# Sums by TensorE in 32-column strips, weight splitting on VectorE, and a new order, in a fused attention and gated MLP kernel

## The chip, the cores and the metric

The kernel runs on one core of a Trainium2 chip. The core has five engines that run side by side, each through its own instructions in order: TensorE (PE, matrix products), VectorE (DVE), ScalarE (ACT), GpSimd (POOL), and SyncE (SP), which here issues the transfers (DMAs). They wait for each other by semaphores. SBUF is the on-chip memory with 128 partitions; PSUM holds what TensorE produces. The metric is the time of one execution on the device in microseconds, the median of several runs. "Busy" times and instruction times come from one execution taken with the hardware profiler.

## The reference

Batch 8, 12 heads, 448 positions, head size 64; model width 768, inner width 1024, all in fp32.

```python
scores = cap * np.tanh(scale * (q @ k.T) / cap)
scores = scores - np.max(scores, axis=-1, keepdims=True)
attn = np.exp(scores)
attn = attn / (np.sum(attn, axis=-1, keepdims=True) + 1e-09)
x = attn @ v                                # heads side by side: (8, 448, 768)
h = np.maximum(x @ w_in, 0.0)               # 768 -> 1024
u, v = h[..., :512], h[..., 512:]
v_n = (v - mean(v)) / np.sqrt(var(v) + 1e-06)          # over the 512
v_s = np.einsum('ts,bsd->btd', w_spatial, v_n) + b_spatial[None, :, None]
out = (u * v_s) @ w_out                     # 512 -> 768
```

The weights w_in and w_out come as float64; cap is a scalar that is known only at run time.

## The kernel before, in words

**Two bodies.** `either` loads cap and the first q, k tiles (`raws`, L902 to L904), keeps TensorE busy with `WARM` = 14 matmuls on zeros (L909), and branches on cap (L920). For a cap up to a bound the body with `bounded=True` runs, the one measured here: the scores are bounded, so exp is taken without subtracting the maximum first, and the maximum only serves the small term 1e-09 in the denominator.

**Attention by quads** (`quad_bnd`). Four heads are one quad; a batch has three, the kernel 24 (`turn` 0 to 23). A q, k tile `raw` holds two heads, 448 columns of q and 448 of k in each partition. For each of the 7 blocks of 64 keys, four 64x64 matmuls (L594), one for each quarter of TensorE's array, make the scores of four heads with the keys on the partitions; ScalarE takes tanh of the block (L598) and exp of two blocks at a time in place (L605) in one of six `tp` buffers; four quadrant matmuls a block (L615) sum the product with v in PSUM (`ps_x`), and ScalarE copies it out (L621).

**Maxima and sums.** For all quads DVE folds the exps of the 7 blocks elementwise (L633), transposes in 32x32 blocks (L641) and reduces (L643), once for the maximum and once for the sum. For the first `PE_SUMS` = 3 quads the sum is made by TensorE instead: quadrant matmuls with a 64x64 tile of ones (L662), accumulated into two PSUM tiles, two ScalarE copies (L671), and four small transfers into `dt` (L674), where the denominators are made (L683, L685). They are written to memory (L686) and read back broadcast (L689), and DVE multiplies (L698). `halves` splits each product into a high part (ACT, L355) and a low part (DVE, L351), both in the reduced format fp32r.

**The MoE part** (`moe`, once a batch) multiplies such split operands in three matmuls per product: with w_in (L754 to L756, L776 to L781), with w_spatial (L845 to L850), with w_out (L870 to L872), on the full 128x128 array. It needs all three quads of its batch and the weights split. For the first of them `FILL` = 8 filler matmuls (L753) come ahead.

**The weights** are loaded as pairs of 32-bit words and turned from float64 into fp32 by `split_f64`: a scaling of the upper word (on GpSimd, L420), three integer steps on DVE (L424, L425, L427), the high part (ACT) and the low part (DVE). `E_W = "PAV"` names the engines of the scaling, the high and the low part. w_in comes in 12 pieces of 512 columns, w_out in 12 of 256; w_spatial, already fp32, in four, with the low parts on GpSimd (L383).

**The order.** Each piece of work is a task with engine, estimated duration, dependences, the buffers it takes and a key. `Plan.order` plays the tasks through once as the program is built: an engine that is free takes, of the tasks that are ready and have buffers, the one with the lowest key; on TensorE a task of the other kind ("R": quadrants, "N": full array) has `STICK` added to its key, and a change costs `TURN`. The order found is fixed in each engine's instruction stream. The keys come from `BND_KEY`, `BND_ADJ` (one for each quad or batch and kind) and `BND_W_KEYS` (the weights).

Of the kernel before, what the change touches and what calls it, by code (L numbers as in the profile page):

```python
# [18 lines left out]
FH = DF // 2  # L19
# [8 lines left out]
def f(ap):  # L28
    return ap.bitcast(F32)
# [13 lines left out]
class Plan:  # L43
# [8 lines left out]
    TURN, STICK = 180.0, 5.6142  # L52
# [131 lines left out]
HW, HH, XL = 400, 620, 50  # L184
# [19 lines left out]
def dve(n):  # L204
    return 1.06 * n + 70
# [40 lines left out]
BND_KEY = dict(ld=20.2062, vld=16.3748, sc=-4.4101, th=2.6266, ex=-12.5751, pv=3.8334, sm=4.9568, mx=1.2536,  # L246
               dn=-1.9573, ev=0.5509, x=0.5743, moe=3.5126, span=11.5964, step=-1.1271, mv=-7.699, vld_=0.5863, sc_=0.1716,
               th_=0.234, ex_=3.1048, pv_=-0.3915, sm_=-0.1418, mx_=1.5249)
BND_ADJ = dict(sc0=-1.9208, sc1=-0.6751, sc2=-0.5665, sc3=0.6591, sc4=1.0022, sc5=0.9243, sc6=0.5641, sc7=3.5286,
               sc8=4.1291, sc9=2.1364, sc10=0.4432, sc11=-0.3562, sc21=1.0782, sc22=-2.0787, sc23=-1.8651, mx0=7.5468, mx1=4.1712,  # L250
               mx2=0.2306, mx3=-3.4986, mx4=-4.2501, mx5=-7.8699, mx6=-6.59, mx7=-4.2274, mx8=-1.6152, mx9=-1.0965, mx10=-2.503,
               mx11=2.4712, mx21=3.6487, mx22=7.5152, mx23=10.1101, sm0=-23.9232, sm1=-5.9121, sm2=-19.3382, sm3=-4.1068,
               sm4=-7.6692, sm5=-6.9113, sm6=-7.6076, sm7=-2.9296, sm8=-4.8786, sm9=-2.9017, sm10=0.1476, sm11=-1.028,
               sm21=7.8004, sm22=5.003, sm23=9.0892, dn0=-13.9326, dn1=2.5665, dn2=1.5054, dn3=3.678, dn4=5.4586, dn5=2.0101,
               dn6=-0.9345, dn7=1.341, dn8=5.2032, dn9=5.9753, dn10=6.5428, dn11=-0.3824, dn21=0.2627, dn22=-7.9155, dn23=32.9005,
               x0=-1.8155, x1=-12.9607, x2=-3.0392, x3=-3.3476, x4=1.7459, x5=0.4945, x6=3.9029, x7=6.1809, x8=0.3782, x9=6.0115,
               x10=5.0057, x11=0.7894, x21=7.5672, x22=-1.7504, x23=1.6104, moe0=-2.1731, moe1=4.7513, moe2=2.8101, moe3=2.4916,
               moe7=9.0071, span0=-2.667, span1=-3.3859, span2=-2.449, span3=-5.6885, span7=28.8127, mv0=4.9503, mv1=-2.4788,
               mv2=2.6326, mv3=3.2084, mv7=-12.8989, wi0=-3.2806, wi1=-21.6066, wi2=-37.6263, wi3=14.5167, wi4=16.5614,
               wi5=1.1376, wi6=13.0344, wi7=2.468, wi8=-18.9783, wi9=3.3202, wi10=-13.2504, wi11=-12.154, ws0=-12.654,  # L260
               ws1=-7.9959, ws2=-33.2129, ws3=-10.2049, wo0=-6.4452, wo1=-0.8201, wo2=2.6051, wo3=8.6589)
BND_V_FIRST = 1
WARM, WARM_N, FILL = 14, 512, 8
BND_W_KEYS = -14.6272, 0.1578, -3.1507, 14.803, -4.1788, 0.5729, 0.2535
SPARE = ()
PE_SUMS = 3
E_W = "PAV"
# [6 lines left out]
def attn_moe(ctx, tc, bounded, shared, qk, v, qk2, v2, cap, w_in, w_sp, w_out, out):  # L274
# [33 lines left out]
    ic, ca, nca, half, raws = shared  # L308
    own = {"raw": list(raws)}
# [63 lines left out]
    def split_f32(key, c):  # L373
# [9 lines left out]
        l = [add("P", gp(S), key, lambda: sub("P", lo[:n], t.t[:n, :S], f(hi[:n])), [b], [t])]  # L383
# [17 lines left out]
    def split_f64(key, src, hi, lo, n, late=False):  # L401


        if late:
            w = y = Buf("xg")
        else:
            w, y = Buf("w64"), Buf("wy")
        y0 = 2 * n if late else 0
# [4 lines left out]
        t = add("S", HW, key, lambda: nc.sync.dma_start(out=w.t.bitcast(U32)[:, :2 * n], in_=src), allocs=[w], lat=dm(128, 8 * n))  # L413
# [18 lines left out]
        for i, (e, d, fn) in enumerate(ops):  # L432
            t = add(e, d, key, fn, [t], [w, y] if i < 4 else [y], [y] if i == 0 and not late else [], name="w64")
# [8 lines left out]
    for j in range(2):  # L442
        for c in range(NP):
            wi_t.append(split_cols((W_KEYS[0] + c * W_KEYS[1], W_KEYS[5] + c * W_KEYS[6])[j] + adj("wi", j * NP + c), j * FH, (j + 1) * FH, lambda key, i, n, c=c, j=j: split_f64(
                key, wi32[c * 128:(c + 1) * 128, 2 * i:2 * n], (wi1_h, wi2_h)[j][:, c, i - j * FH:n - j * FH], (wi1_l, wi2_l)[j][:, c, i - j * FH:n - j * FH], n - i)))
# [119 lines left out]
    def quad_bnd(b, n):  # L565
# [55 lines left out]
        z = add("A", act(PW, 1), kk("ev"), lambda: nc.scalar.copy(out=two(xf.t), in_=x.t[:, :, :S]), [prev], [x, xf], [xf], name="xev")  # L621
# [273 lines left out]
def either(ctx: ExitStack, tc: tile.TileContext, *args):  # L895
# [7 lines left out]
    for i, r in enumerate(raws):  # L903
        nc.sync.dma_start(out=r, in_=args[2][0, i])  # L904
# [14 lines left out]
    shared = ic, ca, nca, half, raws  # L919
# [35 lines left out]
```

## Time and profile before

| | |
|---|---|
| median of 3 runs | 728.85 us (728.6 to 729.24) |
| profiled execution: span, first to last instruction | 726.5 us |
| PE busy | 713.2 us (98%), 4910 matmuls |
| DVE busy | 600.4 us (83%) |
| ACT busy | 479.9 us (66%) |
| POOL busy | 78.4 us (11%) |
| mean granted clock of TensorE | 0.997 |

The profiled execution's own time is its span and what lies around it; the median of the timed runs is 2.35 us longer than the span. Matmuls are pipelined: each is shown with its whole passage through the array, so that PE counts as busy where it could take more, and the spacing of starts says more than the duration of one. An fp32 matmul appears as two matmul records, one in fp32r as one.

### The profile page before, as it was taken

The numbers are of one execution on the slowest core, as the hardware profiler recorded it, in microseconds if no ns is written. First come the engines' busy times: TensorE is split into PE (matmuls) and PEld (weight loads), VectorE is DVE, ScalarE is ACT, GpSimd is POOL, SyncE is SP. The second block draws the span as 40 slices with busy tenths as digits, with TensorE's granted clock in tenths as the row PEclk, the third lists the DMA queues.
The fourth block names the chain that finished last, engine by engine and source line by source line (L and its number), as shares of the span: only waits on it lengthen the run. The fifth ranks groups of instructions, "written<-read, shape, count | busy, mean of one in ns | idle before, by whom it ended". The sixth has DMA issues, their size and how long they took to land.

```text
span 726.5 us, 12274 instructions
## 1 busy us (share of the span) xinstructions
PE 713.2 (98%) x4910; PEld 487.7 (67%) x4910; DVE 600.4 (83%) x849; ACT 479.9 (66%) x648; POOL 78.4 (11%) x71
## 2 busy tenths in 40 slices
PE   8998999999999999999999999999999999999997
PEld 3333576575668657785568688568566865699896
DVE  4899999999999989948999996299799778983520
ACT  6999757849883894649875833786876678424321
POOL 1234310600110001000120001000021000200100
PEclk9999999999999999999999999999999999999999
DMA  8564314524221431033321430124321131202002
GB/s 279 165 204 148 129 38 134 168 80 142 85 78 30 149 129 49 28 91 114 102 76 28 153 103 27 49 66 141 102 77 41 47 131 39 53 2 101 1 1 80
DMA packets 34263, 66.50 MB, mean 92 GB/s; under 512 B 6034, under 2 KB 21908, under 8 KB 34196
## 3 DMA queue, kind: packets, MB, share of 16 engines
q1 hardware_dynamic: 34196, 65.62, 28.3%
q8 instruction: 40, 0.66, 0.4%
q14 instruction: 27, 0.22, 0.1%
HBM read 54.40 MB, written 11.18 MB: 90 GB/s over the span
## 4 chain that ended last, share of the span: by engine, by line
PE 79%; DVE 12%; issue 4%; ACT 2%; DMA 1%; SPq 1%; POOL 0%; DVEq 0%; ACTq 0%; POOLq 0%
PE ps_s L594 13%; PE ps_x L615 13%; PE ps_acc L870 5%; PE ps_acc L871 5%; PE ps_acc L872 5%; PE ps_acc L754 4%; PE ps_acc L756 4%; PE ps_acc L755 4%; DVE red L633 4%; PE ps_acc L779 4%; PE ps_acc L780 3%; PE ps_acc L781 3%; PE ps_acc L848 2%; PE ps_acc L850 2%; PE ps_acc L849 2%
## 5 line engine op out<-in xcount | busy, mean ns | idle before, releaser
L598 ACT ACTIVATE tp<-ps_s,capt 128x896 f32<-128x896 f32 x168 | 162.2, 1003 | 28.6 <-PE ps_s L594 18.1
L633 DVE TENSOR_TENSOR red<-red,tp 128x1792 f32<-128x1792 f32 x90 | 140.9, 1566 | 22.5 <-ACT tp L605 20.8
L605 ACT ACTIVATE tp<-tp,capt 128x1792 f32<-128x1792 f32 (+1 forms) x96 | 154.0, 1606 | 1.5
L594 PE MATMUL ps_s<-raw 64*64 64x448 f32 x1344 | 147.1, 545 | 3.6 <-ACT tp L598 3.5
L615 PE MATMUL ps_x<-tp,v 64*64 64x448 f32 x1344 | 140.0, 536 | 0.5 <-ACT tp L605 0.4
L633 DVE TENSOR_TENSOR red<-tp 128x1792 f32<-128x1792 f32 x45 | 91.2, 2027 | 13.9 <-ACT tp L605 13.0
L615 PEld LDWEIGHTS ps_x<-tp,v 64*64 64x64 f32 x1344 | 51.3, 133 | 75.7 <-issue 68.2
L594 PEld LDWEIGHTS ps_s<-raw 64*64 64x64 f32 x1344 | 47.1, 132 | 80.1 <-issue 46.5
L803 POOL TENSOR_TENSOR lst<-lst,capt 128x1 f32<-128x1 f32 x32 | 34.9, 1091 | 526.7 <-DVE lst L801 482.9
L754 PE MATMUL ps_acc<-xg,wi_h 128*128 128x448 f32 x180 | 66.2, 368 | 0.5 <-ACT xg L355 0.5
L755 PE MATMUL ps_acc<-xg,wi_h 128*128 128x448 f32 x180 | 65.3, 363 | 0.7 <-DVE xg L351 0.6
L756 PE MATMUL ps_acc<-xg,wi_l 128*128 128x448 f32 x180 | 65.2, 362 | 0.0
L870 PE MATMUL ps_acc<-xg,wo_h 128*128 128x448 f32 x176 | 64.5, 367 | 0.0
L871 PE MATMUL ps_acc<-xg,wo_h 128*128 128x448 f32 x176 | 63.7, 362 | 0.6 <-DVE xg L351 0.6
L872 PE MATMUL ps_acc<-xg,wo_l 128*128 128x448 f32 x176 | 63.8, 362 | 0.0
L355 ACT CAST xg<-o 128x448 fp32r<-128x448 f32 x32 | 18.1, 566 | 55.0 <-DVE o L855 49.5
L641 DVE STREAM_TRANSPOSE red<-red 128x896 f32<-128x896 f32 x45 | 49.6, 1102 | 0.7
L779 PE MATMUL ps_acc<-wi_h,xg 128*128 128x512 f32 x126 | 50.1, 398 | 0.0
L643 DVE TENSOR_REDUCE st<-red 128x28 f32<-128x896 f32 x45 | 48.6, 1079 | 0.7
L780 PE MATMUL ps_acc<-wi_l,xg 128*128 128x512 f32 x126 | 49.1, 390 | 0.0
L781 PE MATMUL ps_acc<-wi_h,xg 128*128 128x512 f32 x126 | 49.1, 390 | 0.0
L633 DVE TENSOR_TENSOR red<-red 128x896 f32<-128x896 f32 x45 | 48.6, 1079 | 0.6
(146 smaller groups left out, 1110.1 us busy)
## 6 DMA issues: line engine op xcount, KB each, us to landing
raw<-in_qk SPq DMA_DIRECT2D x48, 448.0 KB
rr<-rd SPq DMA_DIRECT2D x48, 224.0 KB
out<-o SPq DMA_DIRECT2D x48, 224.0 KB
w<-in_w_in SPq DMA_DIRECT2D x12, 512.0 KB
v<-in_v SPq DMA_DIRECT2D x24, 256.0 KB
v<-in_v SPq DMA_DIRECT2D x24, 192.0 KB
xg<-in_w_out SPq DMA_DIRECT2D x12, 256.0 KB
rd<-dt SPq DMA_DIRECT2D x48, 3.5 KB
```

The costliest lines, as they stand in the source:

```text
L594: nc.tensor.matmul(ps.t[c * D:(c + 1) * D, e, :S], lhsT=f(raw[c].t)[r, k:k + D], rhs=f(raw[c].t)[r, :S], start=True, stop=True)
L598: th = add("A", act(PW, 1), kk("th", i), lambda ps=ps, tp=tp, o=o: nc.scalar.activation(out=tp.t[:, o:o + PW].rearrange("p (e q) -> p e q" ...
L605: ex = add("A", act_s(w, 1), kk("ex", i), lambda tp=tp, w=w: nc.scalar.activation(out=tp.t[:, :w], in_=tp.t[:, :w], func=AF.Exp, scale=ca) ...
L615: nc.tensor.matmul(x.t[e * D:(e + 1) * D, c, :S], lhsT=vts[g // 2].t[c * D:(c + 1) * D, (4 * (g % 2) + 2 * j + e) * D:(4 * (g % 2) + 2 * j ...
L633: nc.vector.tensor_tensor(o_(), i0(), i1(), op=op)
L754: nc.tensor.matmul(ps, lhsT=wi1_h[:, c, fs], rhs=x[:, XH:], start=(c == 0), stop=False)
L755: nc.tensor.matmul(ps, lhsT=wi1_h[:, c, fs], rhs=x[:, :S], start=False, stop=False)
L756: nc.tensor.matmul(ps, lhsT=wi1_l[:, c, fs], rhs=x[:, XH:], start=False, stop=(c == NP - 1))
L779: nc.tensor.matmul(ps, lhsT=x[:, XH:][:, ts], rhs=wi2_h[:, c], start=(c == 0), stop=False)
L870: nc.tensor.matmul(ps, lhsT=wo_h[:, c, ns], rhs=g[:, XH:], start=(c == 0), stop=False)
L871: nc.tensor.matmul(ps, lhsT=wo_h[:, c, ns], rhs=g[:, :S], start=False, stop=False)
L872: nc.tensor.matmul(ps, lhsT=wo_l[:, c, ns], rhs=g[:, XH:], start=False, stop=(c == 3))
```

## The change

- **Start.** `WARM` 14 becomes 10. Each of the first two q, k tiles is loaded in two pieces, columns 0 to 639 of both first, then the first piece of w_in (into the tile `red`, which DVE's folds use later), then the other columns of both.
- **Weights.** `E_W` "PAV" becomes "VAV": the scaling of w_in and w_out moves from GpSimd to DVE. The low parts of w_spatial move from GpSimd to DVE as well.
- **Sums.** `PE_SUMS` 3 becomes 4. A sum by TensorE now multiplies all 128 partitions by a 128x32 tile whose column 0 has ones in the upper 64 rows and column 1 in the lower 64, in four matmuls of 224 columns for a block, each into its own strip of 32 PSUM partitions. One ScalarE copy of 224 columns and two transfers per quad follow, where there were two of 448 and four.
- **Order.** `TURN` 180 becomes 120, `STICK` 5.6142 becomes 6.4817, some estimated durations change, and all keys are new, now with one for each quad and batch.

```diff
-    TURN, STICK = 180.0, 5.6142
+    TURN, STICK = 120.0, 6.4817
...
-    return 1.06 * n + 70
+    return 1.04 * n + 70
...
-BND_KEY = dict(ld=20.2062, vld=16.3748, sc=-4.4101, th=2.6266, ex=-12.5751, pv=3.8334, sm=4.9568, mx=1.2536,
+BND_KEY = dict(ld=104.761, vld=34.1706, sc=-4.7, th=131.099, ex=-53.2415, pv=7.4006, sm=6.4322, mx=2.068, dn=-2.9151,
...
-WARM, WARM_N, FILL = 14, 512, 8
+WARM, WARM_N, FILL, HEAD = 10, 512, 8, 192
...
-PE_SUMS = 3
-E_W = "PAV"
+PE_SUMS = 4
+E_W = "VAV"
...
-        one = const.tile([128, D + 80], F32, name="one")[:, :D]
-        nc.gpsimd.memset(one, 1.0)
+        one = const.tile([128, D + 80], F32, name="one")[:, :32]
+        nc.gpsimd.memset(one, 0.0)
+        for c in range(2):
+            nc.gpsimd.memset(one[c * D:(c + 1) * D, c:c + 1], 1.0)
...
-        l = [add("P", gp(S), key, lambda: sub("P", lo[:n], t.t[:n, :S], f(hi[:n])), [b], [t])]
+        l = [add("V", dve(S), key, lambda: sub("V", lo[:n], t.t[:n, :S], f(hi[:n])), [b], [t], name="ws")]
...
-        if late:
+        if first:
+            w = y = Buf("red")
+        elif late:
...
+        if first:
+            t = add("S", 1100, -97, lambda: None, allocs=[w])
...
-            accs, sxs = [Buf("acc"), Buf("acc")], [Buf("u"), Buf("u")]
+            acc, sx, sw = Buf("acc"), Buf("u"), S // 2
 
             def ones(g):
                 for i in range(2 * g, min(2 * g + 2, NB)):
-                    for c in range(2):
-                        for e in range(2):
-                            o = i % 2 * PW + e * S
-                            nc.tensor.matmul(accs[c].t[e * D:(e + 1) * D, 0, :S], lhsT=one[c * D:(c + 1) * D],
-                                             rhs=tps[g].t[c * D:(c + 1) * D, o:o + S], start=(i == 0), stop=(i == NB - 1))
+                    for p in range(4):
+                        o = i % 2 * PW + p * sw
+                        nc.tensor.matmul(acc.t[32 * p:32 * (p + 1), 0, :sw], lhsT=one, rhs=tps[g].t[:, o:o + sw],
+                                         start=(i == 0), stop=(i == NB - 1))
...
+            q = add("A", act(sw), kk("ev"), lambda: nc.scalar.copy(out=sx.t[:, :sw], in_=acc.t[:, 0, :sw]), [s],
+                    [acc, sx], [sx], name="sev")
             for c in range(2):
...
+                outs.append(add("S", HD, kk("dn"), lambda c=c: nc.sync.dma_start(
+                    out=dt.t[64 * c:64 * c + n1, 32:64],
+                    in_=sx.t[c::32, :sw].rearrange("p (b i) -> p b i", i=32)), [q, room], [sx, dt], lat=dm(n1, 128)))
...
-    for i, r in enumerate(raws):
-        nc.sync.dma_start(out=r, in_=args[2][0, i])
+    red = const.tile([128, 2 * PW], F32, name="red")
+    for cols in (slice(0, S + HEAD), slice(S + HEAD, PW)):
+        for i, r in enumerate(raws):
+            nc.sync.dma_start(out=r[:, cols], in_=args[2][0, i][:, cols])
+        if not cols.start:
+            nc.sync.dma_start(out=red.bitcast(U32)[:, :2 * FH], in_=args[5].bitcast(U32)[:128, :2 * FH])
```

## Rows read from the trace of the kernel before

**Rows 1.** Busy time by stretches: PE, PEld, DVE, ACT, POOL (count), clock, DMA share, GB/s.

```profile
40.00:60.00 20.00, 20.00 (x208) 7.28 (x204) 19.93 (x28) 19.31 (x23) 9.73 (x2) 1.00 0.66 209
60.00:80.00 20.00, 15.84 (x107) 8.74 (x100) 19.39 (x31) 18.02 (x27) 6.85 (x6) 0.91 0.37 127
...
80.00:160.00 80.00, 78.95 (x549) 52.11 (x542) 78.89 (x135) 53.67 (x78) 19.71 (x17) 1.00 0.33 104
160.00:720.00 560.00, 560.00 (x3722) 404.31 (x3722) 455.54 (x619) 355.50 (x488) 32.26 (x28) 1.00 0.24 75
```

**Rows 2.** Chain of waits from 160 us: start, us on the chain, engine, tile, line.

```profile
162.38 0.20 PE ps_acc L871
...
162.78 0.91 PE ps_s L594 x8
163.70 1.50 PE ps_x L615 x16
```

**Rows 3.** Timeline of PE from 164 us: start, us, line, operation, shapes, count.

```profile
167.28 1.74 PE L594 MATMUL ps_s<-raw 64*64 64x448 f32 x16
168.94 0.50 PE L779 MATMUL ps_acc<-wi_h,xg 128*128 128x512 f32 x1
169.28 0.40 PE L780 MATMUL ps_acc<-wi_l,xg 128*128 128x512 f32 x1
169.51 0.40 PE L781 MATMUL ps_acc<-wi_h,xg 128*128 128x512 f32 x1
```

**Rows 4.** Groups by line and shape: count, then busy us, mean ns, idle before.

```profile
L662 PE MATMUL ps_acc<-tp,one 64*64 64x448 f32 x168 | 17.7, 537 | 0.9 <-ACT tp L605 0.9
```

**Rows 5.** Timeline of all engines from 0 us, as in rows 3.

```profile
1.17 5.49 PE L910 MATMUL wps<-warm 128*128 128x512 bf16 x14 [1.17 <-DVE capt L913]
...
2.00 0.15 PEld L910 LDWEIGHTS <-warm 128*128 128x128 bf16 x1 [0.28 <-issue]
...
2.43 0.15 PEld L910 LDWEIGHTS <-warm 128*128 128x128 bf16 x1 [0.28 <-issue]
...
6.77 1.73 PE L594 MATMUL ps_s<-raw 64*64 64x448 f32 x16
...
8.39 0.64 POOL L420 TENSOR_SCALAR wy<-w 128x512 f32<-128x512 f32 x1 [0.97 <-DMA w<-in_w_in]
...
9.14 0.43 DVE L424 TENSOR_SCALAR wy<-wy 128x512 uint32<-128x512 uint32 x1 [4.92 <-POOL wy L420]
```

**Rows 6.** Timeline of PE from 58 us, as in rows 3.

```profile
61.72 1.68 PE L594 MATMUL ps_s<-raw 64*64 64x448 f32 x16
66.29 2.62 PE L594 MATMUL ps_s<-raw 64*64 64x448 f32 x16 [2.89 <-ACT tp L598]
...
72.10 0.47 PE L754 MATMUL ps_acc<-xg,wi_h 128*128 128x448 f32 x1 [0.52 <-ACT xg L355]
```

**Rows 7.** DMA view of the first 8 us, in 40 slices of 0.2 us.

```profile
GB/s 0 0 0 0 0 0 0 0 0 0 1 108 36 90 72 54 233 269 376 430 376 484 376 448 376 484 233 108 36 205 266 348 328 369 410 184 287 246 389 389
```

**Rows 8.** Groups by line and shape, as in rows 4: DVE's dense steps.

```profile
L351 DVE TENSOR_TENSOR xg<-xf,xg 128x448 fp32r<-128x448 f32 x48 | 29.1, 629 | 9.8 <-ACT xg L355 9.8
...
L424 DVE TENSOR_SCALAR wy<-wy 128x512 uint32<-128x512 uint32 x12 | 4.8, 414 | 5.5 <-POOL wy L420 5.5
...
L424 DVE TENSOR_SCALAR xg<-xg 128x256 uint32<-128x256 uint32 x12 | 3.2, 277 | 0.1
```

**Rows 9.** The same view of DVE for 0 to 72 us, then 72 to 150.

```profile
L425 DVE SCALAR_TENSOR_TENSOR wy<-w,wy 128x512 uint32<-128x512 uint32 x10 | 7.6, 771 | 0.1
...
L425 DVE SCALAR_TENSOR_TENSOR wy<-w,wy 128x512 uint32<-128x512 uint32 x2 | 1.4, 683 | 0.0
```

**Rows 10.** Busy time of the instructions on tile red, all stretches together.

```profile
sum 727.00, DVE 378.80; mean DVE 189.40
```

**Rows 11.** Two lines of the sums by themselves: group; durations min, median, max.

```profile
L671 ACT COPY u<-ps_acc 128x448 f32<-128x448 f32 x6 | 3.0, 523 | 0.0
...
L674 SPq DMA_DIRECT2D dt<-u x12: 737/764/956, 30.9 to 67.4; - x12
```

More of the change, by code (lines that the diff above doesn't have):

```diff
@@ L306, in make @@
             b.t = dr.tile([4 * S], F32, name=b.tag)
-    ic, ca, nca, half, raws = shared
-    own = {"raw": list(raws)}
+    ic, ca, nca, half, raws, red = shared
+    own = {"raw": list(raws), "red": [red]}
     if bounded:
@@ L319, in keep @@
         def keep(tag, n, width, fill=None):
-            own[tag] = [const.tile([128, width], F32, name=f"{tag}{i}") for i in range(n)]
+            own[tag] = own.get(tag, [])
+            own[tag] += [const.tile([128, width], F32, name=f"{tag}{i}") for i in range(len(own[tag]), n)]
             for t in own[tag]:
@@ L399, in split_f32, with split_f64 @@
         return l
-    def split_f64(key, src, hi, lo, n, late=False):
-        if late:
+    def split_f64(key, src, hi, lo, n, late=False, first=False):
+        if first:
+            w = y = Buf("red")
+        elif late:
             w = y = Buf("xg")
@@ L407, in split_f64 @@
             w, y = Buf("w64"), Buf("wy")
-        y0 = 2 * n if late else 0
+        y0 = 2 * n if w is y else 0
         w3 = lambda: w.t.bitcast(U32)[:, :2 * n].rearrange("p (n t) -> p n t", t=2)
@@ L432, in split_f64 @@
         for i, (e, d, fn) in enumerate(ops):
-            t = add(e, d, key, fn, [t], [w, y] if i < 4 else [y], [y] if i == 0 and not late else [], name="w64")
+            t = add(e, d, key, fn, [t], [w, y] if i < 4 else [y], [y] if i == 0 and w is not y else [], name="w64")
         return t
@@ L444, in attn_moe @@
             wi_t.append(split_cols((W_KEYS[0] + c * W_KEYS[1], W_KEYS[5] + c * W_KEYS[6])[j] + adj("wi", j * NP + c), j * FH, (j + 1) * FH, lambda key, i, n, c=c, j=j: split_f64(
-                key, wi32[c * 128:(c + 1) * 128, 2 * i:2 * n], (wi1_h, wi2_h)[j][:, c, i - j * FH:n - j * FH], (wi1_l, wi2_l)[j][:, c, i - j * FH:n - j * FH], n - i)))
+                key, wi32[c * 128:(c + 1) * 128, 2 * i:2 * n], (wi1_h, wi2_h)[j][:, c, i - j * FH:n - j * FH], (wi1_l, wi2_l)[j][:, c, i - j * FH:n - j * FH], n - i,
+                first=bounded and not (j or c))))
     for c in range(4):
@@ L620, in quad_bnd @@
         two = lambda y: y.rearrange("p (c q) -> p c q", q=S)
-        z = add("A", act(PW, 1), kk("ev"), lambda: nc.scalar.copy(out=two(xf.t), in_=x.t[:, :, :S]), [prev], [x, xf], [xf], name="xev")
+        z = add("A", act(PW), kk("ev"), lambda: nc.scalar.copy(out=two(xf.t), in_=x.t[:, :, :S]), [prev], [x, xf], [xf], name="xev")
         by_pe = turn < PE_SUMS
@@ L648, in quad_bnd @@
             o = slice((2 * c + 1) * 32, (2 * c + 2) * 32)
-            d = [add("A", 145, kk("dn"), lambda p=p, o=o: nc.scalar.copy(out=sh.t[p, :32 * len(done)], in_=st.t[o, :32 * len(done)]), d,
+            d = [add("A", 300, kk("dn"), lambda p=p, o=o: nc.scalar.copy(out=sh.t[p, :32 * len(done)], in_=st.t[o, :32 * len(done)]), d,
                      [st, sh], [sh] if c == 0 else [], name="shift")]
@@ L918, in either @@
     nc.vector.tensor_scalar(nca, ca, -1.0, None, op0=ALU.mult)
-    shared = ic, ca, nca, half, raws
+    shared = ic, ca, nca, half, raws, red
     with tc.If(bits <= CAP_BITS) as cmp:
```

55 lines of the change are left out of this document (29 added, 26 removed).

## The prediction, made before the result was known

> **What bounds the kernel now.** Profiled span 726.5 us; the timed median, 728.85, lies 2.35 above it. I keep that distance, so a change of the span is a change of the median.
>
> I read the busy time by stretches first [rows 1]. From 80 us on TensorE (PE) is busy without a break. VectorE (DVE) is full too from 40 to 160 us (78.9 of 80 us after the 80th) and slack later (455.5 of 560). Before 80 us there is one hole: from 60 to 80 PE starts 107 matmuls and its clock is granted 0.91.
>
> "Busy" hides pipelining, so I counted PE's work by spacing. The chain of waits shows PE alone after 160 us [rows 2]: a 448-column full-array matmul every 0.20 us, and 16 quadrant (64x64) matmuls in 1.50 us, 0.094 each, four at a time in 0.375. A 512-column one takes 0.23 [rows 3]. Counts come from the loops: an fp32 matmul stands in the trace as two, so the 24 quads give 24x7x8 = 1344 for the scores and 1344 for the product with v; 168 more are the sums [rows 4]; the MoE part has 8x(72+44+72) = 1504 of 448 columns and 8x66 = 528 of 512; 8 are filler. So 252.0 + 15.8 + 302.4 + 121.4 = 691.6 us of work. It starts at 6.77 us [rows 5], and some 5 us of copy and store follow the last matmul. 726.5 - 6.8 - 691.6 - 5 leaves 23 us in which PE turns round or waits.
>
> Two parts of the 23 us can be placed. Changing between quadrants and the full array costs on the way in 0.91 for 8 matmuls instead of 0.75, and on the way out 1.66 for 16 instead of 1.50, then 0.34 instead of 0.23 [rows 2, 3]: 0.16 + 0.27, about 0.4 us a pair. And the hole: the scores issued at 61.72 are through at 63.4, the next start at 66.29, behind a wait of 2.9 us for ScalarE's tanh; they run slowly (2.62 for 16); the first MoE matmul waits until 72.10 [rows 6]. That is some 7 us where work for the MoE part is late, and what is late is made by DVE and ScalarE (ACT), busy 19.9 and 19.3 of the 20 us before [rows 1].
>
> So the kernel is PE's work, plus what the start-up costs because three full engines feed each other.
>
> **The change part by part.** (a) *Start.* Fourteen warm-up matmuls hold PE from 1.17 to 6.66 us, and the first score follows at 6.77 [rows 5]. Ten, 0.43 apart, end at 5.44. The 0.92 MB of the first two q, k tiles come in between 3.2 and 5.2 us at about 400 GB/s [rows 7]; the first 640 of 896 columns, now sent first, need 0.66 MB and land 0.65 us earlier. With 0.1 us to start, the first score is at 5.5: -1.25. Bounds: 0 (the lower clock lasts into the scores, 0.75 us per group of 8 more, which eats it) to -1.25. The w_in piece that now stands between (0.52 MB, 1.3 us) pushes the last 256 columns of q, k to about 7 us; the fourth score needs them, two tanh (2 us) after the first, so this costs nothing by a small margin.
>
> (b) *Weights on DVE.* The first step of the split leaves GpSimd. Today the first piece reaches GpSimd at 8.39, DVE at 9.14 [rows 5]; ahead of the branch it lands near 6.2, so DVE can start near 6.5: -2.6 us for DVE (bounds 0 and -2.6). DVE gains twelve scalings of 512 and twelve of 256 columns. No row shows this step on DVE; the dense shift takes 0.414 and 0.277 [rows 8], a two-source step 0.68 [rows 9]. I take the first as nearest (one source), 5.0 + 3.3, and 8.2 + 4.1 as upper end; added work cannot gain by itself. Four low parts of w_spatial go over at 0.63 [rows 8]: 2.5. Sum +10.8 (to 14.8).
>
> GpSimd's work stretched DVE's: the same step means 0.771 before 72 us, 0.683 after [rows 9], 0.9 us over ten, and as much for its twin line; -1.8 (bounds 0 and twice that). That GpSimd itself is spared only shortens a chain.
>
> (c) *Sums.* A sum that stays on DVE costs it one fold: 378.8 us over 45, 8.4 each [rows 10]. The fourth quad's goes: -8.4. DVE in all: 10.8 - 8.4 - 1.8 - 2.6 = -2.0 us, between +6.4 (upper price, nothing recovered) and -3.8.
>
> On PE, three quads of quadrant sums are 168 x 0.094 = 15.8 us. The new form multiplies all 128 rows into a strip of 32 columns, half the moving columns, four strips per step. No row shows it. If four strips run together as four quadrants do, a group takes half of 0.375: 4 quads x 14 groups x 0.188 = 10.5 us, -5.3. If the pace is instructions rather than columns, the quadrants' 0.375 per four is the slow end the rows give: 21.0, +5.3. I take -5.3: the columns set the pace of every form in rows 2 and 3.
>
> The strips break the run of quadrant matmuls. The old sums had the same 64x64 shape as their neighbours and cost no turn; the new ones lie in some 13 places (16 tasks, a few adjacent). Per place the bounds are nothing and the 0.4 us of quadrants against full array [rows 2, 3]; I take the middle, as only part of the geometry changes: +2.6 (0 to +5.2). The Trainium skill, TensorEngine Tiling (Array Packing), under Key Properties, says that changing the tiling mode, unlike changing the tile, drains TensorE. By that rule each of the 13 places pays, and if it pays in full the strips bring nothing (-5.3 + 5.2); no row here has this pair of modes.
>
> ACT evacuates one half-width sum per quad in place of two at 0.52 [rows 11], at least -1.6 over the first three (one at the full price each); two small transfers per quad in place of four at 0.76 of issue each, so the denominators of the first batch come some 1.5 us earlier. Other queues: the q, k, v and weight loads behind them on SP gain the same. DVE's normalisation waits for these transfers; what is late next there is DVE itself.
>
> (d) *Order.* All priorities are new, with no term that can be counted. What it can reach is the 23 us: from -7 (the hole closed) to +4 (PE's shorter work turns into waiting, since the feeders are no faster). I credit 2 us, because DVE delivers 2.0 earlier and ACT about as much.
>
> **Sum.** -1.25 (start) - 5.3 (sums) + 2.6 (turns) - 2.0 (waits) = -5.95: span 720.6, time **722.9 us**.
>
> **The rivals.** *The hole closes too.* For: 7 us of PE waiting sit in one place, and every engine that feeds it gets lighter or earlier. Against: DVE stays full to 160 us. Its price: 5 us beyond the 2 credited, 718, or 716 with turns that cost nothing.
>
> *The relief becomes waiting.* The sums lie where ACT and DVE are full; if these do not deliver earlier, PE merely idles longer before the MoE part: only the start remains and the fourth quad's 2.6 us on PE is new, within 1.4 of 728.85. Against: DVE loses 8.4 us of fold.
>
> *The strips do not overlap* (the other side, slower). Its place is each group of four, its price 21.0 us of sums for 15.8, with turns 5.2 + 5.2 - 1.25 = +9.2 and the 2 us not gained: about 736 at most, 733 with half the turns. With turns at 2.6 it decides from 0.26 us per group on: 56 x 0.26 = 14.4 = 15.8 + 1.25 - 2.6. For: eight instructions (four loads, four matmuls) then must go in 0.188 us, twice the pace any row shows. Against: nothing in the quadrants' rows shows that instructions limit them.
> The Trainium skill, TensorE: Matmul & The Clock Gate, "Wait — 56ns, not 53.3ns?", gives about 62 ns per matmul as sequencer time when hardware decode is off. A group would then take 0.248, the sums 13.9 us, 3.4 more than I take: 726.3, still faster; the quadrants' 94 ns neither show nor exclude it.
>
> *DVE becomes the bound.* With the dearer scaling and neither the earlier start nor the stretch recovered it has up to 6.4 us more before 160 us: 731 to 733. Against: the first piece does land earlier.
>
> **How the numbers follow.** Forecast, 719.5 to 727: 0.47, the skill's issue pace within it. Hole closed, below 719.5: 0.25. Relief into waiting: 0.10. Strips: 0.11. DVE: 0.07. About 0.2% (1.5 us) is what a measurement of this kernel can tell from no change. Faster is the first two and a little of the third (0.74), same the rest of the third (0.09), slower the last two nearly whole (0.17). The range 713 to 731.5 leaves out 0.03 below and 0.13 above.
>
> **What would show it.** Right: the first score near 5.5 us and DVE's first weight step near 6.5; a group of four strips starting every 0.19 us; GpSimd without weight work; the hole before the first MoE matmul shorter; PE from then on without gaps. Wrong: strips 0.3 us or more apart per group, a gap of 0.4 on each side of them, DVE still working without a pause when PE waits after 80 us, or more mode changes after 160 us than now, which only the new order could bring.

## The result, and the profile after

723.35 us median (722.52 to 723.76, 4 runs), the kernel before beside it 728.73 (727.82 to 729.24): ratio 0.992, 95% interval 0.9906 to 0.9934. The forecast was 722.9 us. The profiled span fell from 726.5 to 722.0 us. The number came out, in part by luck: some of the working behind it did not, and the experiments show which part.

The stretches of the kernel after, columns as in [rows 1]:

```profile
0.00:20.00 20.00, 15.43 (x106) 5.52 (x110) 12.06 (x26) 12.51 (x14) 0.99 (x13) 0.91 0.81 284
20.00:40.00 20.00, 19.54 (x240) 7.25 (x236) 18.51 (x28) 19.54 (x22) 0.00 (x0) 1.00 0.67 220
40.00:60.00 20.00, 18.75 (x208) 6.20 (x207) 19.46 (x32) 19.43 (x23) 0.00 (x0) 1.00 0.51 145
60.00:80.00 20.00, 17.51 (x195) 7.73 (x195) 18.95 (x31) 19.55 (x27) 0.00 (x0) 1.00 0.53 169
80.00:160.00 80.00, 80.00 (x558) 54.03 (x554) 77.93 (x150) 56.69 (x85) 3.02 (x4) 1.00 0.36 115
160.00:720.00 560.00, 556.88 (x3683) 404.77 (x3675) 450.04 (x611) 350.35 (x480) 22.66 (x28) 1.00 0.23 73
```

The first two stretches of the kernel before, which [rows 1] do not have:

```profile
0.00:20.00 20.00, 17.36 (x134) 6.92 (x138) 9.60 (x18) 13.52 (x14) 4.50 (x15) 1.00 0.79 268
20.00:40.00 20.00, 19.62 (x208) 7.34 (x204) 17.09 (x23) 19.37 (x23) 5.35 (x6) 1.00 0.56 178
```

Against these and [rows 1] the hole of 60 to 80 us is shallower (17.51 busy with 195 matmuls, was 15.84 with 107; clock 1.00, was 0.91), but TensorE is busy less from 0 to 20 us (15.43, was 17.36) and from 40 to 60 (18.75, was 20.00), and its clock is 0.91 in the first 20. From 20 to 80 us GpSimd (fifth busy column) has nothing left to do, and ScalarE (the fourth) is at 19.4 to 19.6 of 20. The last stretch ends on copy and store, so its 556.88 is no sign of new pauses.

TensorE's first 25 us in the kernel after (start, us, line, shapes, count, wait):

```profile
5.34 2.30 PE L611 MATMUL ps_s<-raw 64*64 64x448 f32 x16
...
13.78 2.16 PE L632 MATMUL ps_x<-tp,v 64*64 64x448 f32 x16 [1.95 <-DMA v<-in_v]
15.70 3.01 PE L611 MATMUL ps_s<-raw 64*64 64x448 f32 x16
...
20.89 0.96 PE L678 MATMUL ps_acc<-tp,one 128*32 128x224 f32 x16
21.79 0.98 PE L611 MATMUL ps_s<-raw 64*64 64x448 f32 x8
```

The first score is at 5.34 us (6.77 in [rows 5]). Then two things that I had not foreseen: a wait of 1.95 us for v, whose transfer stands behind w_in pieces, and 16 scores that take 3.01 us at the lower of the clock's two levels, 1.2 GHz (granted 0.50 from 15.0 to 18.3 us), instead of 1.68 [rows 6]. The strips are as forecast: four start within 20 ns, the next four 0.189 us after the first (0.188 forecast). A place (a run of strips among the quadrant matmuls) of 16 strips takes 20.89 to 21.79, 0.90 for 0.754 of work, and the four quadrant matmuls before it 0.486 us for 0.375: about 0.25 us of turning. Ten of the 13 places show the same two figures; with as much in all 13 it is 3.3 us (2.6 forecast). The Trainium skill, TensorEngine Tiling (Array Packing), Key Properties, says that a change of the tiling mode drains TensorE; the trace agrees, at 0.25 us a place. The Trainium skill, TensorE: Matmul & The Clock Gate, "Wait — 56ns, not 53.3ns?", gives about 62 ns per matmul for the case that hardware decode is off. That pace is not met here: four strips start every 0.189 us, 47 ns each, and the measurement decides.

VectorE (DVE) in the kernel after: the first weight step, then, of the groups in the first 160 us, weight steps (the busy time, then the mean ns of one):

```profile
7.62 0.43 DVE L436 TENSOR_SCALAR red<-red 128x512 f32<-128x512 f32 x1 [3.18 <-SPq L968]
```

```profile
L443 DVE SCALAR_TENSOR_TENSOR wy<-w,wy 128x512 uint32<-128x512 uint32 x11 | 7.5, 685 | 0.1
...
L441 DVE SCALAR_TENSOR_TENSOR wy<-w,wy 128x512 uint32<-128x512 uint32 x11 | 7.4, 674 | 0.0
...
L436 DVE TENSOR_SCALAR wy<-w 128x512 f32<-128x512 f32 x11 | 4.6, 417 | 1.0 <-DMA w<-in_w_in 1.0
L436 DVE TENSOR_SCALAR xg<-xg 128x256 f32<-128x256 f32 x12 | 3.4, 283 | 0.0
```

The scalings cost 12 x 0.417 + 12 x 0.283 = 8.4 us (8.3 forecast). The two-source steps take 0.67 to 0.69 where they took 0.76 in the same window before ([rows 9]: 0.771 early, 0.683 later): without GpSimd's work beside them the stretch is gone. The first weight step is at 7.62 us, 1.5 earlier than before, where I had 2.6; the releaser that its row names is SyncE, not the transfer.

**The chain of waits.** The share of each engine and line in it from 20 to 80 us, of the kernel before and then after (the view cuts such a line at its end):

```profile
by line: DVE red L633 27.2%; issue 8.8%; DVE wy L425 6.8%; DVE red L641 5.2%; DVE wi_l L351 5.1%; SPq L674 5.1%; DVE wy L427 5.1%; DMA wy<-in_w_sp 4.0%; DVE xg L351 3.7%; DVE st L643 3.7%; ACT wi_h L355 3.6%; ACT tp L598 3.2%; DVE wy L424 3
```

```profile
by line: ACT tp L615 16.0%; PE ps_s L611 15.8%; ACT tp L622 15.8%; PE ps_x L632 14.2%; PE ps_acc L678 8.1%; DMA rr<-rd 7.1%; DMA rd<-dt 5.7%; ACT xf L638 4.3%; ACT xg L366 3.4%; SPq L593 2.5%; issue 1.8%; ACT wi_h L366 1.7%; SPq L704 1.1%; 
```

Added up piece by piece, VectorE had 39.6 of these 60 us before and 0.6 after; TensorE had none and now has 22.7, ScalarE (ACT) went from 7.1 to 25.4. By this chain VectorE paced the start-up, and after the change it no longer does. The chain names who came last, not by how much: e12 below shows how far it can be read.

One instruction serves as a milestone: DVE's multiplication of the first batch's third quad, which the first MoE product needs. Before and after:

```profile
84.82 1.15 DVE L698 TENSOR_TENSOR xf<-xf,rr 128x448 f32<-128x448 f32 x2
```

```profile
79.44 1.15 DVE L713 TENSOR_TENSOR xf<-xf,rr 128x448 f32<-128x448 f32 x2
```

5.4 us earlier; the median of the runs gained 728.73 - 723.35 = 5.4, the span 4.5. VectorE by itself up to there, before and then after (length, busy, count, clock, DMA share, GB/s):

```profile
0.00:84.82 84.82, 70.25 (x103) 0.98 0.59 193
```

```profile
0.00:79.44 79.44, 68.42 (x111) 0.98 0.63 206
```

Its idle time ahead of the milestone went from 14.6 to 11.0 us, its busy time from 70.3 to 68.4. Before, the fourth quad's sum fold does not lie in this part: its steps start between 90.50 and 99.23 us, as in these two rows of its timeline.

```profile
90.50 2.02 DVE L633 TENSOR_TENSOR red<-tp 128x1792 f32<-128x1792 f32 x1
...
99.23 1.08 DVE L643 TENSOR_REDUCE st<-red 128x28 f32<-128x896 f32 x1
```

### The profile page after: what moved, and what is told of

Read it like the earlier page. It is cut to its first block, busy times and chain, and to the rows that moved or that the text cites. A ratio compares the mean times of both kernels' runs of the same rounds, so it can differ in the third digit from the quotient of the medians.

```text
span 722.0 us, 12333 instructions
## 1 busy us (share of the span) xinstructions
PE 708.1 (98%) x4962; PEld 485.5 (67%) x4962; DVE 597.0 (83%) x870; ACT 478.1 (66%) x646; POOL 26.7 (4%) x45
## 4 chain that ended last, share of the span: by engine, by line
PE 92%; ACT 4%; DMA 2%; SPq 0%; issue 0%; DVE 0%; ACTq 0%
PE ps_x L632 16%; PE ps_s L611 16%; PE ps_acc L885 5%; PE ps_acc L769 5%; PE ps_acc L771 5%; PE ps_acc L770 5%; PE ps_acc L886 5%; PE ps_acc L887 5%; PE ps_acc L794 4%; PE ps_acc L795 4%; PE ps_acc L796 4%; PE ps_acc L863 3%; PE ps_acc L865 2%; PE ps_acc L864 2%; PE ps_acc L791 2%; PE ps_acc L792 2%
## 5 line engine op out<-in xcount | busy, mean ns | idle before, releaser
L622 ACT ACTIVATE tp<-tp,capt 128x1792 f32<-128x1792 f32 x96 | 154.2, 1609 | 1.3
L611 PE MATMUL ps_s<-raw 64*64 64x448 f32 x1344 | 148.8, 547 | 3.0 <-ACT tp L615 2.9
L650 DVE TENSOR_TENSOR red<-red,tp 128x1792 f32<-128x1792 f32 x88 | 136.5, 1551 | 14.9 <-ACT tp L622 13.4
L650 DVE TENSOR_TENSOR red<-tp 128x1792 f32<-128x1792 f32 x44 | 88.9, 2020 | 16.9 <-ACT tp L622 16.1
L366 ACT COPY o<-ps_acc 128x448 f32<-128x448 f32 x44 | 23.4, 532 | 41.1 <-PE ps_acc L887 28.5
L818 POOL TENSOR_TENSOR lst<-lst,capt 128x1 f32<-128x1 f32 x32 | 25.7, 803 | 652.2 <-DVE lst L816 647.7
```

The lines of the kernel that those rows point to most:

```text
L611: nc.tensor.matmul(ps.t[c * D:(c + 1) * D, e, :S], lhsT=f(raw[c].t)[r, k:k + D], rhs=f(raw[c].t)[r, :S], start=True, stop=True)
L622: ex = add("A", act_s(w, 1), kk("ex", i), lambda tp=tp, w=w: nc.scalar.activation(out=tp.t[:, :w], in_=tp.t[:, :w], func=AF.Exp, scale=ca) ...
L650: nc.vector.tensor_tensor(o_(), i0(), i1(), op=op)
```

## The experiments

Each is an edit of the kernel after that keeps its order of instructions, unless it says otherwise. Differences "to after" are differences of the ratios to the kernel before, times 728.73; both ratios have an interval of about 1 us to each side, so such a difference is known to some 1.5 us.

| run | median us | ratio (95%) | to after, us | milestone, us | span, us |
|---|---|---|---|---|---|
| after | 723.35 | 0.992 (0.9906, 0.9934) | | 79.44 | 722.0 |
| e1 one block | 722.16 | 0.9911 (0.9896, 0.9927) | -0.7 | 77.36 | 719.9 |
| e2 double | 726.71 | 0.9967 (0.9955, 0.9979) | +3.4 | 81.44 | 725.2 |
| e3 quadrant shape | 721.86 | 0.99 (0.9885, 0.9915) | -1.5 | 77.57 | 720.0 |
| e4 v first | 723.98 | 0.9933 (0.9918, 0.9948) | +0.9 | 78.47 | 722.3 |
| e5 weights back | 724.3 | 0.9949 (0.993, 0.9967) | +2.1 | 78.77 | 721.6 |
| e6 old start | 722.99 | 0.9921 (0.9908, 0.9934) | +0.1 | 78.42 | 721.1 |
| e9 fourth fold | 732.79 | 1.0041 (1.0027, 1.0055) | +8.8 | 88.00 | 731.8 |
| e10 tanh twice | 726.09 | 0.995 (0.9937, 0.9963) | +2.2 | 81.83 | 724.8 |
| e11 fold twice | 726.22 | 0.9956 (0.9943, 0.9969) | +2.6 | 80.89 | 724.0 |
| e12 high on GpSimd | 724.71 | 0.9935 (0.9922, 0.9948) | +1.1 | 79.78 | 722.9 |

From the milestone to the end every one of them needs 642.4 to 643.8 us. So all but some 1.4 us of what these edits do to the time is done by then. Milestone and span are those of one execution each, which need not be a middling one: e5's is its fastest.

**Is TensorE's work before 80 us on the path? (e1, e2, e8)** e1 sums only the last block:

```diff
-                for i in range(2 * g, min(2 * g + 2, NB)):
+                for i in range(NB - 1, min(2 * g + 2, NB)):
...
-                                         start=(i == 0), stop=(i == NB - 1))
+                                         start=True, stop=True)
```

> The changed kernel (723.35 us) with its sums over the last block of 64 keys alone: 8 strip matmul records per quad instead of 56, in 4 places instead of 13, everything else in the same order; the denominators are therefore wrong. It takes 192 records of 0.047 us and 9 places of 0.25 us from TensorE's start-up, 9.0 + 2.3 = 11.3 us. Theory A (TensorE's work and turns between 5 and 75 us are on the path): 712 us. Theory B (ScalarE and VectorE set the pace there, what TensorE saves becomes waiting): 722 to 723.5 us.

Measured: 0.7 us less, where TensorE lost 11.3 us of work and turns. Two rows of its stretches show it idle (15.46 of 20 us), with VectorE and ScalarE (third and fourth busy column) at 19.3 to 19.9:

```profile
20.00:40.00 20.00, 16.85 (x176) 5.67 (x172) 19.29 (x29) 19.90 (x23) 0.00 (x0) 1.00 0.71 231
40.00:60.00 20.00, 15.46 (x152) 4.57 (x144) 19.72 (x31) 19.85 (x24) 0.00 (x0) 1.00 0.55 155
```

e2 issues each strip matmul twice (`for again in range(2):` around the four).

> The changed kernel with every strip matmul issued twice, so that the sums are twice as large; no new place and no new turn, the same order. It adds 224 records of 0.047 us, 10.5 us, to TensorE's start-up. Theory A (on the path): 734 us. Theory B (the added work lies in waits): 723.5 to 726 us.

Measured: +3.4 us for 10.5 of work; the chain from 20 to 80 us then goes over TensorE:

```profile
by line: PE ps_s L611 24.4%; PE ps_acc L679 23.3%; PE ps_x L632 21.1%; DMA rr<-rd 7.7%; DMA rd<-dt 6.5%; ACT tp L615 3.6%; ACT xg L366 3.4%; ACT tp L622 2.8%; issue 1.5%; ACT xf L638 1.5%; SPq L593 1.1%; SPq L705 1.1%; DVE xf L714 1.1%; SPq
```

e8 is the kernel before, in its order, with the strips for its three quads:

```diff
-                    for c in range(2):
-                        for e in range(2):
...
+                    for p in range(4):
+                        o = i % 2 * PW + p * sw
+                        nc.tensor.matmul(accs[0].t[32 * p:32 * (p + 1), 0, :sw], lhsT=one, rhs=tps[g].t[:, o:o + sw],
...
```

> The kernel before with nothing but the sums of its three quads in strips (one copy of 224 columns and two transfers for each), in the order of before. TensorE loses 15.8 - 7.9 us and gains about 10 places of 0.25 us: -5.4; ScalarE loses 0.5 to 0.7 per quad. Theory A (TensorE's path): 723.3 us. Theory B (ScalarE and VectorE pace the start-up): 726.5 to 728.5 us.

Measured: 727.85, ratio 0.9988 (0.9978 to 0.9997): 0.9 us less than the kernel before (0.2 to 1.6), for 7.9 us of matmuls saved on TensorE less ten turns of 0.25, 5.4. Its chain stays on VectorE:

```profile
by line: DVE red L635 20.5%; DVE wy L427 8.0%; issue 7.7%; DMA rd<-dt 7.5%; DMA rr<-rd 6.6%; DMA xg<-in_w_out 6.4%; DVE wy L429 6.1%; DVE wi_l L353 6.0%; DVE red L643 5.2%; DMA wy<-in_w_sp 4.9%; DVE xf L700 3.9%; DVE wy L426 3.8%; DVE xg L3
```

So the saving on TensorE that I counted in full is worth about a sixth of it in the old order. In the new order TensorE has about 7 us of room upwards (10.5 less 3.4, e2), and taking work from it gives nothing that can be told from 0 (e1).

**The turns (e3).** The sums as two quadrant matmuls of half width, the same time on TensorE without a change of shape (half of the columns are left out of the sums):

```diff
-                    for p in range(4):
-                        o = i % 2 * PW + p * sw
+                    for c in range(2):
+                        p, o = slice(c * D, (c + 1) * D), i % 2 * PW + c * sw
...
```

> The changed kernel with each block's four strips (128 rows by 32 columns, 224 moving columns) replaced by two diagonal 64x64 quadrant matmuls of 224 columns: the same TensorE time per block (0.375 us), but the shape of the neighbouring matmuls, so no change of tile shape; half of the columns are left out of the sums, which are therefore wrong. Theory A (the 13 turns of 0.25 us are paid on the path): 3.3 us less, 720.1 us. Theory B (start-up paced by the other engines): 723.3 us. If the turn is not a matter of the shape, the 0.11 us before and the 0.14 us behind each place stay in the trace.

Measured: 1.5 us less, at the edge of the noise, for 3.3 us of turns. Its trace shows that the turn is a matter of the shape:

```profile
17.36 0.93 PE L611 MATMUL ps_s<-raw 64*64 64x448 f32 x8
18.11 0.73 PE L678 MATMUL ps_acc<-tp,one 64*64 64x224 f32 x5
18.50 0.59 PE L611 MATMUL ps_s<-raw 64*64 64x448 f32 x2
```

The sums start 0.75 us after the eight scores ahead of them, the bare price of eight, where the strips needed 0.86 (20.03 to 20.89), and the next scores start among the sums.

**The start (e4, e6).** e4 issues the first quad's v ahead of three w_in pieces.

> The changed kernel with the two loads of the first quad's v issued ahead of the next three pieces of w_in behind the branch, all else in the same order. In the changed kernel TensorE waits 1.95 us for that v at 11.8 us and then has the lower clock from 14.9 to 18.4 us. Theory A (TensorE's path): the wait and the lower clock go, 1.9 + 1.7 us, about 720 us. Theory B (the first 20 us are bound by the transfers, and VectorE waits for its weight pieces 1.1 us longer instead): 723 to 724.5 us.

Measured: no gain (+0.9). Its milestone is 1.0 us earlier, its end no earlier: the wait for v shows no cost in the end. e6 takes the old start: 14 warm-up matmuls, the first tiles whole, no weight piece ahead of the branch.

> The changed kernel with the start of before: 14 warm-up matmuls, the first q, k tiles loaded whole, the first piece of w_in loaded behind the branch; all else in the same order. Theory A: the first score comes 1.43 us later and with it everything: 724.8 to 725.3 us. Rival: the loads of v and of the weights, which land at the same time either way, hide the earlier start: 723.5 us.

Measured: the same time as after (0.9921 against 0.992), though its first score and its first weight step are late:

```profile
1.18 4.77 PE L926 MATMUL wps<-warm 128*128 128x512 bf16 x14 [1.18 <-DVE capt L929]
6.05 1.81 PE L611 MATMUL ps_s<-raw 64*64 64x448 f32 x16
...
9.87 0.43 DVE L436 TENSOR_SCALAR red<-red 128x512 f32<-128x512 f32 x1 [5.69 <-DMA red<-in_w_in]
```

My theory of a loss of 1 to 2 us fell, though its test is weaker than planned. The first score is late by 0.71 us and not by 1.43, because here the 14 warm-up matmuls took 4.77 us where they took 5.49 [rows 5]; why is not shown. So about half of the 1.43 us between the kernels before and after seems to belong to the executions, not to the change. VectorE's first weight step, at least, is 2.25 us later than in the kernel after (7.62), and the milestone is no later (78.42, was 79.44): the early start is taken up before 80 us.

**The weights' engine (e5).** Scaling and the low parts of w_spatial back on GpSimd:

```diff
-                eng[E_W[0]].tensor_scalar(yf(), i, 2.0 ** -112, 1.0, op0=ALU.mult, op1=ALU.mult)
+                nc.gpsimd.tensor_scalar(yf(), i, 2.0 ** -112, 1.0, op0=ALU.mult, op1=ALU.mult)
...
-        l = [add("V", dve(S), key, lambda: sub("V", lo[:n], t.t[:n, :S], f(hi[:n])), [b], [t], name="ws")]
+        l = [add("V", dve(S), key, lambda: sub("P", lo[:n], t.t[:n, :S], f(hi[:n])), [b], [t], name="ws")]
```

> The changed kernel with the scaling of w_in and w_out and the low parts of w_spatial on GpSimd again, in the same order of work. So far the sums' form has shown little on the path (a seventh of the strips: 1.2 us less; twice the strips: 3 us more), so ScalarE and VectorE should pace the start-up. Theory B1 (VectorE's busy time paces it, the split's engine hardly matters): VectorE loses 10.8 us of work, of which some 7 before 80 us, and gets 2 to 3.4 of stretching back: 719 to 721 us. Theory B2 (a weight piece that waits on GpSimd, 1.2 us in the mean and up to 9 when VectorE holds the port, comes late to ScalarE and VectorE, whose queues are in order): 725 to 729 us. If neither: 723.5.

Measured: +2.1 by the ratio, +1.0 by the medians, with runs from 723.37 to 727.84: between the two theories, and hardly clear of noise. The profiled run is the fastest one, as fast as after, so its rows can't show the loss; they show why there is no gain. VectorE has 6.6 us less to do ahead of the milestone and yet is busy 69.28 us up to there, more than after (68.42). Among its folds in the same stretch, e5 and then after, this group took the most of it, and the chain goes back to VectorE:

```profile
L650 DVE TENSOR_TENSOR red<-red 128x896 f32<-128x896 f32 x4 | 7.0, 1753 | 0.0
```

```profile
L650 DVE TENSOR_TENSOR red<-red 128x896 f32<-128x896 f32 x4 | 4.3, 1068 | 0.0
```

```profile
by line: DVE red L650 21.9%; PE ps_x L632 12.0%; PE ps_s L611 9.8%; issue 7.5%; DVE wy L443 5.8%; ACT tp L622 5.7%; ACT tp L615 5.3%; DVE red L658 5.1%; PE ps_acc L678 5.1%; DVE wy L441 3.9%; ACT xg L366 3.2%; ACT wi_h L366 2.1%; DVE wi_l L
```

**The order (e7).** The kernel after with the keys, `TURN` and `STICK` of before, so that the order is made anew.

> The changed kernel with the keys and the two constants of before, so that the order is planned anew from the old keys; strips, four sums, the weights on VectorE and the early start stay. My prediction credits the order with 2.0 us: 725.5 us. Rival (with the start-up paced by ScalarE and VectorE, TensorE's relief is worth little and the order brought most of the gain): 727 to 730 us. Other rival (the parts bring it, any order will do): 723.5 us.

Measured: 749.5 us, ratio 1.0281 (1.0268 to 1.0294), 26 us slower than after and beyond every theory; the chain goes over VectorE and transfers:

```profile
by line: DVE red L642 20.4%; issue 12.0%; DMA wy<-in_w_sp 10.3%; DMA rr<-rd 8.3%; DVE wi_l L354 6.1%; DVE wy L433 6.0%; DVE wy L435 5.2%; DVE red L650 5.2%; DMA rd<-dt 3.9%; DVE xf L705 3.9%; DVE st L652 3.7%; DVE wy L432 3.0%; DVE wy L428 
```

It shows that the old keys do not fit the new parts, not what the new keys are worth alone; the kernel before in the new order was not run.

**Which engine paces the start-up now? (e9 to e12)** e9 issues the six VectorE steps of the fourth quad's maximum twice, folds, transpose and reduce alike:

```diff
-                nc.vector.tensor_tensor(o_(), i0(), i1(), op=op)
+                for _ in range(2 if turn == 3 else 1):
+                    nc.vector.tensor_tensor(o_(), i0(), i1(), op=op)
...
```

> The kernel after, with the six VectorE steps of the fourth quad's maximum (four folds, transpose, reduce) each issued a second time with the same result: VectorE gets back the 8.4 us of the fold that the change took from it with the fourth quad's sum, at the place where it lay; TensorE's and ScalarE's work and the order stay. Base: the kernel after, 0.992 of the kernel before, about 723.4. Theory A (VectorE's load up to 160 us sets the end, so the fold's 8.4 us is where the gain of the change comes from): +6 to +8, 729.5 to 731.5. Theory B (ScalarE sets the pace of the start-up, VectorE has room): +0 to +2, 723.4 to 725.4. Theory C (they hand the work to each other, each late part counts in part): +3 to +5.

Measured: +8.8, a little above theory A. TensorE has run out of other work and waits for the third quad's split product, and the 448-column matmuls are 0.37 us apart instead of 0.20, at the lower clock (granted 0.50 from 89 to 95 us). Of its timeline:

```profile
89.27 0.74 PE L770 MATMUL ps_acc<-xg,wi_h 128*128 128x448 f32 x1 [3.46 <-ACT xg L366]
92.28 0.74 PE L771 MATMUL ps_acc<-xg,wi_h 128*128 128x448 f32 x1 [2.27 <-DVE xg L362]
92.82 0.57 PE L772 MATMUL ps_acc<-xg,wi_l 128*128 128x448 f32 x1
93.19 0.57 PE L770 MATMUL ps_acc<-xg,wi_h 128*128 128x448 f32 x1
```

The multiplication that they wait for stands behind the doubled fold in VectorE's order: 88.00 us instead of 79.44. In one point the expectation is wrong: this is not the place where the sum's fold lay (90 to 100 us, behind the milestone). So e9 gives the price of VectorE's work directly ahead of the milestone, one for one, and not what the fold's removal brought. It is not the price everywhere ahead of it: e11 puts 4.0 us in earlier and pays 2.6.

e10 and e11 add 4.0 us to one engine in the second quad, tanh and fold issued twice:

```diff
+                for _ in range(2 if turn == 1 and i < 4 else 1):
+                    nc.scalar.activation(out=tp.t[:, o:o + PW].rearrange("p (e q) -> p e q", q=S), in_=ps.t[:, :, :S],
...
+                for _ in range(2 if turn == 1 and wide else 1):
+                    nc.vector.tensor_tensor(o_(), i0(), i1(), op=op)
```

> The kernel after, with the second quad's first four tanh each issued twice with the same result: about 4.0 us more on ScalarE between 20 and 40 us, all else kept. Theory A (VectorE sets the pace): 0 to +1, 723.4 to 724.4. Theory B (ScalarE sets the pace of the start-up): +3.5 to +4.5, 727 to 728. Theory C (both in turn): about +2, 725 to 726. TensorE's account alone would say 0, since TensorE waits there anyway.

> The kernel after, with the two wide folds of the second quad's maximum each issued twice with the same result: about 4.0 us more on VectorE between 35 and 45 us, all else kept. Theory A (VectorE sets the pace): +3.5 to +4.5, 727 to 728. Theory B (ScalarE sets it): 0 to +1, 723.4 to 724.4. Theory C (both in turn): about +2, 725 to 726.

Measured: +2.2 and +2.6. Theory C fits both best, though with 1.4 us to each side the near edges of the other theories are not all excluded. The chain goes to the engine that was loaded (ScalarE 41.1 of the 60 us in e10, VectorE 21.9 in e11); e10, then e11:

```profile
by line: ACT tp L617 33.0%; ACT tp L626 20.7%; PE ps_s L611 9.5%; PE ps_x L636 8.8%; issue 7.3%; PE ps_acc L682 6.6%; ACT xg L366 4.2%; ACT xf L642 4.2%; ACT wi_h L366 3.8%; ACT sh L670 1.4%; ACT u L690 1.3%
```

```profile
by line: DVE red L651 15.1%; ACT tp L622 12.8%; PE ps_x L632 11.3%; PE ps_s L611 9.7%; ACT tp L615 9.4%; issue 5.3%; PE ps_acc L679 4.6%; ACT xg L366 4.4%; DVE wy L443 4.1%; DVE red L659 3.4%; DVE wy L441 3.1%; ACT xf L638 2.7%; DVE ws_l L3
```

e12 relieves ScalarE: GpSimd makes w_in's high parts.

```diff
-            (E_W[1], ct(E_W[1], n), lambda: copy(E_W[1], hi, yf())),
+            (E_W[1], ct(E_W[1], n), lambda: copy("A" if late else "P", hi, yf())),
```

> The kernel after, with the high parts of w_in (12 copies of 512 columns) made by GpSimd in place of ScalarE, in the same order: ScalarE loses about 12 x 0.62 = 7.4 us, nearly all before 80 us. Theory B (ScalarE sets the pace): 3 to 5 us less, 718.5 to 720.5, a version that beats both kernels. Theory A (VectorE sets the pace): no change or up to 2 us more, 723.4 to 725.4, since VectorE's low parts then wait for a slower engine and its steps beside GpSimd take longer. Theory C: about 1 to 2 us less, 721.5 to 722.5.

Measured: +1.1, no version that beats the kernel after. The group on GpSimd, in the first 160 us, takes 1.56 us a copy where ScalarE took 0.617, and the chain goes over VectorE and GpSimd:

```profile
L370 POOL TENSOR_SCALAR wi_h<-wy 128x512 fp32r<-128x512 f32 x11 | 17.1, 1559 | 65.2 <-DVE wy L443 65.2
```

```profile
by line: DVE red L650 17.4%; POOL wi_h L370 12.4%; issue 11.3%; DMA rr<-rd 6.5%; DVE wy L441 6.0%; DMA rd<-dt 5.9%; DVE wy L443 5.3%; DVE red L658 5.1%; DVE wi_l L362 4.6%; DVE xg L362 3.7%; DVE st L660 3.6%; DVE ws_l L362 3.4%; DVE xf L713
```

VectorE has 37.7 of the 60 us here, nearly what it had before (39.6), and the kernel is still only about 1 us slower than after. In e3 it has 20.9, at a time no longer than that of after. So its leaving the chain is not in itself the 5.4 us: three engines end close together, and a small push decides which of them the chain shows.

## Why the number was right, and which steps were not

**What bounds the kernel.** Half right. I read the hole before the first MoE matmul as the feeders' fault, VectorE's and ScalarE's; the chain of before puts 39.6 of 60 us on VectorE. But I then summed as if TensorE's work before 80 us were on the path.

**(a) Start, -1.25.** The first score moved by 1.43 (1.25 forecast), of which e6 leaves 0.71 to the change, and the end by nothing that shows (e6, to 1.4 us). The step failed in taking a gain of TensorE at the start for a gain at the end.

**(b) Weights on DVE.** The prices held: scalings 8.4 against 8.3, the stretch's end 12 x (0.756 - 0.674) + 12 x (0.757 - 0.685) = 1.8 against 1.8. Only the earlier first piece gave 1.5 instead of 2.6 us, and e6 shows that it was not needed. Moving the work back gains nothing and may cost 1 to 2 us (e5), though VectorE is spared some 10.8: on GpSimd it stretches VectorE's other steps. "DVE becomes the bound" (731 to 733) is refuted.

**(c) Sums, -5.3 and +2.6.** The sizes were right: the strips overlap, and by spacing TensorE's work fell by 5.2 us; the turns were 3.3. "The strips do not overlap" is refuted (its ceiling was added up wrongly besides: 728.85 + 9.2 with nothing gained is 738, not 736). The step that failed is their place. Strips alone gain 0.9 (e8), and turns given back gain 1.5 of 3.3, at the edge of the noise (e3). For TensorE, "the relief becomes waiting" was the true account, and its condition, that the other engines deliver no earlier, is what did not hold.

**(d) Waits, -2.0.** Too small, and the reason half right. VectorE does come to the milestone earlier, by 5.4 us, but not because its work ahead of it shrank by my sum: with each group's mean duration it is 75.9 us both times. The scalings (10 x 0.417), w_spatial's low parts (2.5) and the end of the fourth quad's maximum (2.2) came in, 8.8 in all; the stretch beside GpSimd (4.6, counting folds and casts that I had left out) and weight steps of one to two pieces (4.2), which the new order puts behind the milestone, went out. What shrank is its idle time (by 3.6), and its steps overlap more (1.8 us less busy for the same sum). Of the 3.6, 1.5 lie ahead of the first weight step and 2.0 behind it. The part ahead was not what counted, nor was the wait for GpSimd's scaling: of its 5.5 us in [rows 8], 4.92 lie there too [rows 5], and e6 waits 5.69 in their place and still reaches the milestone at 78.42. These are VectorE's rows from its first weight step to the milestone, before and then e6:

```profile
9.14:84.82 75.68, 69.46 (x97) 0.98 0.58 190
```

```profile
9.87:78.42 68.55, 67.19 (x105) 1.00 0.64 205
```

Behind that step VectorE idles 6.2 us in the kernel before, 4.2 in the one after and 1.4 in e6.

Behind the milestone the fold's 8.4 us are gone and as much weight work came in, 4.2 + 2 x 0.417 + 12 x 0.283 = 8.4 (the maximum's end, 2.2, went ahead), and TensorE is fed there as before: 641.7 us from the milestone to the end before, 642.5 after. My step failed in setting the fold against the scalings as if both lay on one stretch.

So -5.95 was near -5.4 by luck, because errors cancelled: start, strips and turns, -3.95 in the sum, were worth perhaps 1 us, and VectorE's earlier arrival, -2.0 in the sum, nearly all. "The hole closes too" came half true: by the spacing of its starts, turns counted in, TensorE's idle time of 60 to 80 us fell from some 7 us to 4, and that of 20 to 60 grew from some 2 to 5.5.

**Why no more.** The chain went from VectorE to ScalarE and TensorE in turns, and these end nearly as late: 4.0 us more on ScalarE or on VectorE cost 2.2 and 2.6 (e10, e11), less on TensorE gives nothing that the interval separates from 0 (e1), and what ScalarE hands to GpSimd is lost there (e12).

**What stays open.** By exclusion (start 0, strips about 1, the weights' engine 1 to 2, each known to some 1 to 2 us) the rest, some 3 us give or take 2.5, lies in the room that the fold left behind the milestone together with the order that uses it. That was argued from the rows, not shown: the kernel before in the new order, and a fold put back behind the milestone, were not run. e7 shows that new parts in the old keys lose 26 us.

## What to carry to other kernels

Where three engines are each over 90% busy in one stage, read who holds the chain of waits there before crediting any of them: here taking 5.4 us from one that was off the chain gained 0.9. But take the chain as a list of suspects, not of prices: e12 has VectorE on it as long as the kernel before, and is about 1 us from after. Find the instruction that ends the stage and add up each engine's work ahead of it and behind it apart: 8.4 us more directly ahead of it cost 8.8, 4.0 us more in an earlier quad 2.6, and a term that doesn't move it was worth nothing here, however well it was priced. And count a relief only up to the next engine's chain, which a doubled instruction on that engine measures.

## What the runs showed of the hardware

Strip matmuls of 128x32 run four at a time like quadrants, one group of 224 columns every 0.189 us, but cost 0.25 us of turning per place among 64x64 matmuls; the same sums in 64x64 shape showed no such turn (e3). TensorE's granted clock fell after it had waited: after the pauses of the first 13 us in the kernel after (0.50 from 15.0 to 18.3 us), and in e9 within the wait of 3.46 us, behind which the 448-column matmuls started 0.37 us apart instead of 0.20. Beside GpSimd's steps a VectorE fold of 128x896 took 1.75 us on average instead of 1.07 (e5). A GpSimd copy to fp32r of 128x512 took 1.56 us (e12) where ScalarE's took 0.617.
